# Scores of the early odd units written to the feed-forward banks, early maxima moved to one tile of their own

## The chip, the core and the metric

The kernel runs on one core of a Trainium2 chip. The core has a matmul engine (PE, with a separate weight-load track PEld), three engines for element-wise work (DVE, ACT, POOL), a queue engine (SP) that issues all transfers here, and DMA engines. The metric is the device time of one execution in microseconds, given as the median of several runs.

## What is computed

Pooled attention with 8 batches and 8 heads of 64 columns, followed by a feed-forward layer whose activation is `h * cos(h)`. Queries are averaged in pairs, so 576 pooled queries meet 1152 keys per head.

```python
def _attn_ref(q, k, v):
    B, H, S, D = q.shape                      # 8, 8, 1152, 64
    q_pool = q.reshape(B, H, S // 2, 2, D).mean(axis=3)
    scores = np.matmul(q_pool, k.transpose(0, 1, 3, 2)) / np.sqrt(D)
    scores = scores - np.max(scores, axis=-1, keepdims=True)
    attn = np.exp(scores)
    attn = attn / (np.sum(attn, axis=-1, keepdims=True) + 1e-09)
    return np.matmul(attn, v)
...
    x = attn_out.transpose(0, 2, 1, 3).reshape(B * S // 2, H * D)   # 4608 x 512
    h = x @ w_in                                                    # w_in 512 x 2048
    return (h * np.cos(h)) @ w_out                                  # w_out 2048 x 512
```

## The kernel before, in words

**Pairs and units.** Heads are taken two at a time: 32 pairs, `p` = 0 to 31. Each pair has ten units of attention work, so 320 units `u`, with `p, i = divmod(u, 10)`. Nine units of a pair are wide: four matmuls of 512 columns write the scores of two blocks of 128 keys into one PSUM tile `st` of two banks (`s_unit`, L1217). One unit of a pair is the remainder (64 queries per head, many matmuls of 64 columns, `s_rem`, L1240), the sixth of a pair in the first three pairs and the first of a pair after that. After the scores ACT takes the exponential of the whole tile out of PSUM (`soft`, L1267), and one unit later PE multiplies the result by the values (`av`, L1293 and L1342), accumulating in `ava` and `avb`.

**Maxima.** The exponent needs the row maximum of the scores, which enters as an additional row of the second query part `q2T`. So before a pair's scores PE computes a cheaper version of them from `q1T` alone, DVE reduces it to maxima, ACT writes them beside the second query part (L991 or L1063), and a transposing DMA makes `q2T` (L994 or L1067). In the first three pairs (`NHW` = 3) this goes head by head: four calls of `head_main` and one `head_rest` per head, then `mx_mixed` and `mx_mixed_rest`. The last of these also spreads the value maximum of the pair, from which ACT scales the pair's values (`prep_v`, L1106) before its first `av`.

**Banks.** The kernel lays out eight PSUM banks of 512 fp32 columns: `st` and `mx` are one tile of two banks each, `f` is two tiles of one bank each, `ava` and `avb` are one bank each. A tile is reused in the order in which the program takes tiles of that name, once the last reader of the one before has finished. `f` is the bank of the feed-forward tiles; before the feed-forward starts it holds the weight maxima (`wam`), the third part of the remainder scores in the first four pairs, and some of the early maxima: with `NMXF` = 2, of the calls of `head_main` for pair 1 every second one (`two`) takes two `f` tiles instead of `mx`.

**Order.** The body is written once in program order. `arrange` then takes the recorded instructions and sets each engine's order by a list schedule: it keeps a clock per engine, costs for each instruction, and always places the ready instruction with the lowest place in the program. A change between matmul tile shapes adds a fixed cost on PE. Each engine works through its own order strictly, waiting on semaphores.

**Feed-forward.** Weights are loaded and decoded early (DVE L518, L521, L524, ACT L531, L558, L559, POOL L562). When the four pairs of a batch are done, its rows go through `ffn1` (L1553, into `f`) and `ffn2` (L1613), interleaved with the units of later pairs. Thirty-two pairs' units and 18 chunks of feed-forward work share PE from then on.

Of the kernel before, what the change touches and what calls it, by code (L numbers as in the profile page):

```python
# [9 lines left out]
F32 = mybir.dt.float32  # L10
# [4 lines left out]
AF = mybir.ActivationFunctionType  # L15
# [5 lines left out]
P = 128  # L21
# [29 lines left out]
SRATE = (1.0, 0.6)  # L51
EWR = 2
NMIX = 5
NMXF = 2
NREM = 4
SIN2 = 1
VACT = 6
# [87 lines left out]
def n_out(wr):  # L145
    return wr[0][2] if wr else 1


def arrange(tc, nc, extra, fill):
# [3 lines left out]
    for i in rec:  # L153
        rd, wr = boxes(i)
        eng = str(i.engine).split(".")[-1]
        if eng == "PE":
# [15 lines left out]
            c = max(n_out(wr) * 0.0004167 + 0.0025, 0.0295)  # L172
            if rd[0][4] == 4:
                c = 2 * max(n_out(wr) * 0.00167 + 0.0025, 0.112)
# [21 lines left out]
    for k, nd in enumerate(nodes):  # L196
        deps = set()
        for w, lst in ((0, nd["rd"]), (1, nd["wr"])):
            for t, box, *_ in lst:
                name = t.name  # L200
                if name not in hist:
                    hist[name] = ([], [], set())
                    tag = getattr(t, "tag", None)
# [39 lines left out]
    for a, b, *kind in extra:  # L243
        a, b = node_of[a], node_of[b]
# [35 lines left out]
    while total:  # L280
        best = None
        for e in engines:
            while wait[e] and wait[e][0][0] <= now[e]:
                heapq.heappush(avail[e], heapq.heappop(wait[e])[1])
            if avail[e]:
                cand = (now[e], avail[e][0], e)
            elif wait[e]:
                cand = (wait[e][0][0], wait[e][0][1], e)
            else:
                continue  # L290
            if best is None or cand < best:
                best = cand
        t0, (_, k), e = best
        if avail[e]:
            heapq.heappop(avail[e])
        else:
            heapq.heappop(wait[e])
        nd = nodes[k]
        if nd["lock"]:
            t0 = max(t0, lock)  # L300
        c = nd["cost"]
        if e == "Activation":
            f = "sin" if "Sin" in nd["func"] else "exp" if "Exp" in nd["func"] else table
            if f != table:
                c += 1.28
                table = f
        if e == "PE" and nd["tile"] != mode:
            c += 0.15
            mode = nd["tile"]
        end = t0 + c  # L310
        if nd["lock"]:
            lock = end
        now[e] = end
        fin = end + HAND.get(e, 0.06)
        if e == "SP":
            if nd["cost"] > 1.0:
                end = now[e] = max(end, dma_free - 1.0)
            dma_free = max(dma_free, end) + nd["dma"]
            fin = dma_free + nd["lat"]
        done[k] = fin  # L320
        order[e].append(k)
        total -= 1
        for j in users[k]:
            r = done[k] if nodes[j]["eng"] != e or e == "SP" else end
            if (k, j) in issue:
                r = end
            if nodes[j]["eng"] == "SP" and e != "SP":
                r += SPM
            ready[j] = max(ready[j], r)
            left[j] -= 1  # L330
            if not left[j]:
                heapq.heappush(wait[nodes[j]["eng"]], (ready[j], nodes[j]["key"]))
# [18 lines left out]
def tile_attention_ffn(  # L351
# [10 lines left out]
    nc = tc.nc  # L362
# [18 lines left out]
    exp_scale = 0.5 / math.sqrt(D)  # L381
    l_add = math.log(PMAX)
# [10 lines left out]
    psum = ctx.enter_context(tc.tile_pool(name="psum", bufs=1, space=PSUM))  # L393
# [243 lines left out]
    def kcol(n, t, j, h):  # L637
        if n == 0:
            return t[:, (h * KT + j) * P : (h * KT + j + 1) * P]
        js = J0 if j < RB else J1  # L640
        return kpart(t, js)[:, h, j - js.start]
# [114 lines left out]
    def mx_main(n, t, c):  # L756
        if n not in mxs:
            mxs[n] = sb2.tile([P, NSL, 3], F32, tag="mxs", name="mxs")
        mx_n[0] += 1
        two = n < NMXF and mx_n[0] % 2  # L760
        banks, m = first_tile(2, None if two else "mx")
# [79 lines left out]
    def head_main(h, t):  # L841
        def fn(n):
# [4 lines left out]
            mx_n[0] += 1  # L847
            two = n < NMXF and mx_n[0] % 2
            banks, whole = first_tile(2, None if two else "mx")
# [61 lines left out]
    def first_tile(two, main):  # L911
        if main:
            m = psum.tile([P, 2, 512], F32, tag=main, name="m0")
            return [m[:, 0], m[:, 1]], m
        return [psum.tile([P, 512], F32, tag="f", bufs=2, name="m0") for _ in range(two)], None
# [273 lines left out]
    st = {}  # L1189

    def jof(p, i):
        nf = nf_of(p)
        if not 0 < nf < KT:
            return i - 1
        n = min(nf, KT - nf)
        seq = [x for a in range(n) for x in (a, nf + a)]
        return (seq + list(range(n, nf)) + list(range(nf + n, KT)))[i - 1]

    def banks_of(p, i):
        if p < NHW:  # L1200
            x = 2 * (i if i < FREM else i - 1)
            return [divmod(y, KT) for y in (x, x + 1)]
        return [(h, jof(p, i)) for h in range(2)]

    def is_rem(p, i):
        return i == (0 if p >= NHW else FREM)

    def s_unit(u):
        if u >= NP * NU:
            return  # L1210
        p, i = divmod(u, NU)
        ka, kb, qa, qb = k1[p % 3], k2[p % 2], q1T[p], q2T[p]
        if not is_rem(p, i):
            s = psum.tile([P, 2, 512], F32, tag="st", name="st")
            for y, (h, j) in enumerate(banks_of(p, i)):
                for w, x, part in ((ka, qa, 0), (kb, qb, 1)):
                    nc.tensor.matmul(  # L1217
                        s[:, y, :].rearrange("p (t c) -> p t c", c=P),
                        kcol(p, w, j, h),
                        x[:, h * QT : (h + 1) * QT, :],  # L1220
                        start=part == 0,
                        stop=part == 1,
                        skip_group_check=True,
                    )
            st[u] = [(s.rearrange("p a c -> p (a c)"), 2 * 512)]
            return
        st[u] = [s_rem(p, 0, JR, "st")]

    def s_rem(p, j0, j1, tag):
        ka, kb, qa, qb = k1[p % 3], k2[p % 2], q1T[p], q2T[p]  # L1230
        if tag == "f":
            s = psum.tile([P, 512], F32, tag=tag, bufs=2, name=tag).unsqueeze(1)
        else:
            s = psum.tile([P, 2, 512], F32, tag=tag, name=tag)
        for j in range(j0, j1):
            r = j - j0
            for h in range(2):
                for w, x, part in ((ka, qa, 0), (kb, qb, 1)):
                    o = (r % RB) * P + h * D
                    nc.tensor.matmul(  # L1240
                        s[:, r // RB, o : o + D],
                        kcol(p, w, j, h),
                        x[:, 2 * QT + (h if part == 0 else 0), HALF[h]],
                        start=r % RB == 0 and h == 0 and part == 0,
                        stop=False,
                        skip_group_check=True,
                    )
        n = (j1 - j0) * P
        return s.rearrange("p a c -> p (a c)")[:, 0:n], n

    def soft(u):
        p, i = divmod(u, NU)
        nf = nf_of(p)
        src = st.pop(u)
        rem = is_rem(p, i)
        if rem:
            src.append(s_rem(p, JR, KT, "f" if p < NREM else "mx"))
        parts = {}
        j0 = 0 if rem or p < NHW else jof(p, i)
        for s, n in src:  # L1260
            js = range(j0, j0 + n // P) if rem else [j0]
            f = sum(j < nf for j in js)
            full = n > P
            tag = ("pp" if full else "pps") if f else ("e" if full else "es")
            nb = (NPP if f else NE) if full else 1
            e = sb2.tile([P, n], F32, tag=tag, bufs=nb, name=tag)
            nc.scalar.activation(e, s, AF.Exp, scale=exp_scale, bias=l_add)  # L1267
            pp, c0 = None, 0
            if f < len(js):
                c0 = f * P  # L1270
                tag = "pp" if full else "pps"
                pp = sb2.tile([P, 2, n], F16, tag=tag, bufs=NPP if full else 1, name=tag)
                nc.scalar.copy(pp[:, 0, c0:n], e[:, c0:n])  # L1273
                if full and u % DSH == DSH - 1 and u >= DFIRST:
                    nc.vector.tensor_sub(pp[:, 1, c0:n], e[:, c0:n], pp[:, 0, c0:n])  # L1275
                else:
                    for o in range(c0, n, 512):
                        c = slice(o, min(o + 512, n))
                        nc.gpsimd.tensor_sub(pp[:, 1, c], e[:, c], pp[:, 0, c])  # L1279
            for a, j in enumerate(js):  # L1280
                w = slice(a * P, (a + 1) * P) if rem else slice(0, n)
                parts[j] = (e[:, w], None) if j < nf else (pp[:, 0, w], pp[:, 1, w])
            j0 += n // P
        return parts
# [518 lines left out]
    for u in range(NUNITS):  # L1803
        p, i = divmod(u, NU)
# [12 lines left out]
        while credit > 0.0:  # L1817
            c = next(ffn, None)
# [74 lines left out]
```

## Time and profile before

| | us |
|---|---|
| median of 3 runs | 1529.35 (1526.34 to 1531.48) |
| the profiled execution | 1525.26 |
| its span, first to last instruction | 1523.4 |
| PE busy | 1490.2 (98% of the span) |
| ACT busy | 1172.4 (77%) |
| DVE busy | 1124.1 (74%) |
| POOL busy | 929.6 (61%) |

The span is read first: 1.9 us of the execution lie outside it. Busy time of PE overstates its work a little, since the shown length of one matmul includes the time its result takes to drain while the next already runs. So a wait on PE shows as idle time only for the part that is longer than that overlap. What ended an idle stretch is named behind an arrow.

### The profile page before, as it was taken

The page shows a single profiled execution, that of the slowest core. Times are in us where ns is not written, and L with a number is a line of the kernel's source. Part 1 is how long each engine was busy: PE and PEld are TensorE (multiplying, and loading weights), DVE is VectorE, ACT ScalarE, POOL GpSimd, SP SyncE. Part 2 cuts the span into 40 slices and gives each one's busy share as a digit, 9 for nine tenths or more (in the row PEclk, how much of TensorE's full clock was granted, in tenths as well). Part 3 has the DMA queues.
Part 4 walks back from the last instruction along what each step waited for, and adds up shares of the span by engine and source line. Part 5 has one row for each costly group of instructions (what it writes and reads, how often), then busy time and mean ns, then how long its engine had stood idle before and what let it go on. Part 6 is the DMA issues. An engine that isn't in the chain of part 4 may idle for free.

```text
span 1523.4 us, 39324 instructions
## 1 busy us (share of the span) xinstructions
PE 1490.2 (98%) x16774; PEld 1027.2 (67%) x16774; DVE 1124.1 (74%) x1556; ACT 1172.4 (77%) x1475; POOL 929.6 (61%) x806
## 2 busy tenths in 40 slices
PE   5999999999999999999999999999999999999998
PEld 3777787657666676666666657667666667666665
DVE  7898987777888788887867887878787875343332
ACT  4877689888988788887968887988888787864442
POOL 4644757886665858686555586676767665521222
PEclk9999999999999999999999999999999999999999
DMA  9978742635354433535333334454453321001000
GB/s 264 273 219 181 177 93 48 125 78 116 70 102 102 108 89 76 128 79 123 73 75 79 73 83 107 86 104 103 80 120 83 80 56 32 17 19 32 20 16 22
DMA packets 226111, 145.15 MB, mean 95 GB/s; under 512 B 202448, under 2 KB 204752, under 8 KB 223888
## 3 DMA queue, kind: packets, MB, share of 16 engines
q1 hardware_dynamic: 225936, 142.65, 40.5%
q8 instruction: 131, 2.15, 0.6%
q14 instruction: 44, 0.36, 0.1%
HBM read 74.45 MB, written 10.49 MB: 56 GB/s over the span
## 4 chain that ended last, share of the span: by engine, by line
PE 88%; DVE 5%; ACT 3%; issue 1%; DMA 1%; POOL 1%; SPq 0%; ACTq 0%; DVEq 0%; POOLq 0%
PE f L1553 20%; PE f L1613 19%; PE st L1217 15%; PE ava L1293 8%; PE avb L1293 6%; PE m L765 6%; PE st L1240 2%; PE mx L1613 1%; DVE mxs L779 1%; PE ava L1342 1%; PE st L1553 1%; PE mx L808 1%; PE mx L787 1%; PE avb L1553 1%; PE mx L1553 1%
## 5 line engine op out<-in xcount | busy, mean ns | idle before, releaser
L1279 POOL TENSOR_TENSOR pp<-e,pp 128x512 f16<-128x512 f32 x374 | 457.3, 1244 | 270.6 <-ACT pp L1273 141.9
L1553 PEld LDWEIGHTS <-w 128*128 128x128 f16 x3456 | 331.4, 98 | 61.7 <-issue 3.0
L1553 PE MATMUL f<-xT,w 128*128 128x256 f16 x3048 | 366.2, 273 | 0.3 <-DVE y L1581 0.2
L1267 ACT ACTIVATE e<-st 128x1024 f32<-128x1024 f32 x267 | 272.5, 1020 | 109.9 <-PE st L1217 84.1
L779 DVE TENSOR_REDUCE mxs<-m 128x2 f32<-128x1024 f32 x232 | 283.2, 1221 | 97.1 <-PE m L765 95.0
L1613 PE MATMUL f<-w,g 128*128 128x512 f16 x1440 | 333.2, 380 | 0.7 <-DVE y L1581 0.7
L1503 POOL TENSOR_TENSOR g<-hsc,g 128x512 f16<-128x512 f32 x144 | 192.0, 1355 | 162.1 <-ACT g L1502 160.4
L1273 ACT CAST pp<-e 128x1024 f16<-128x1024 f32 x267 | 278.9, 1045 | 9.8 <-PE ava L1293 2.1
L1293 PEld LDWEIGHTS <-pp 128*128 128x128 f16 (+1 forms) x7062 | 238.8, 100 | 64.2 <-issue 12.5
L1613 PEld LDWEIGHTS <-g 128*128 128x128 f16 x1680 | 158.5, 98 | 177.3 <-DVE y L1581 0.9
L1217 PE MATMUL st<-q1T,k 128*128 128x512 f16 x576 | 218.8, 380 | 4.4 <-ACT pp L1267 4.1
L1293 PE MATMUL ava<-vc,pp 128*128 128x65 f16 (+5 forms) x4502 | 218.9, 198 | 1.3 <-DVE lx L1407 1.2
L1217 PE MATMUL st<-q2T,k 128*128 128x512 f16 x576 | 218.5, 379 | 0.0
L1293 PE MATMUL avb<-vc,pp 128*128 128x65 f16 (+1 forms) x3052 | 179.3, 197 | 0.0
L1217 PEld LDWEIGHTS <-k 128*128 128x128 f16 x1152 | 104.8, 98 | 100.9 <-issue 11.2
L1491 DVE TENSOR_TENSOR hsc<-hsc,y 128x512 f32<-128x512 f32 x144 | 134.8, 976 | 25.3 <-ACT y L1485 25.1
L1577 ACT ACTIVATE hsc<-f,small 128x512 f32<-128x512 f32 x127 | 86.7, 683 | 83.6 <-PE f L1553 83.2
L1581 DVE SCALAR_TENSOR_TENSOR y<-f,r1a,y 128x512 f32<-128x512 f32 x127 | 94.6, 745 | 66.1 <-ACT y L1580 61.3
L765 PE MATMUL m<-k,q1T 128*128 128x512 f16 x464 | 138.1, 379 | 2.5 <-DVE mxs L779 2.0
L1275 DVE TENSOR_TENSOR pp<-e,pp 128x1024 f16<-128x1024 f32 x80 | 127.5, 1593 | 16.7 <-ACT pp L1273 16.2
L1502 ACT CAST g<-hsc 128x512 f16<-128x512 f32 x144 | 83.0, 613 | 11.6 <-PE f L1613 11.6
L696 POOL TENSOR_TENSOR kst<-kld,kst 128x1152 f16<-128x1152 f32 x30 | 75.5, 2516 | 20.9 <-ACT kst L695 20.9
(189 smaller groups left out, 1853.6 us busy)
## 6 DMA issues: line engine op xcount, KB each, us to landing
vld<-in_v_dram SPq DMA_DIRECT2D x32, 576.0 KB, 3.8
kld<-in_k_dram SPq DMA_DIRECT2D x30, 576.0 KB, 4.5
qld<-in_q_dram SPq DMA_DIRECT2D x30, 576.0 KB, 4.6
k<-k SPq DMA_DIRECT2D x31, 288.0 KB, 3.5
wraw<-in_moe_w_in_dram SPq DMA_DIRECT2D x8, 1024.0 KB, 8.0
wraw<-in_moe_w_out_dram SPq DMA_DIRECT2D x8, 1024.0 KB, 6.1
out_dram<-ob SPq DMA_DIRECT2D x32, 256.0 KB, 2.4
left<-lx SPq DMA_DIRECT2D x64, 16.0 KB, 2.0
```

The lines of the kernel that those rows point to most:

```text
L765: nc.tensor.matmul(banks[h], q1T[n][:, h * QT + t, :], kmain(n, k1[n % 3], c, h), start=True, stop=True, skip_group_check=True,),
L779: nc.vector.reduce_max(mxs[n][:, t : t + QT + 1 : QT, c], m, axis=AX.X)
L1217: nc.tensor.matmul(s[:, y, :].rearrange("p (t c) -> p t c", c=P), kcol(p, w, j, h), x[:, h * QT : (h + 1) * QT, :], start=part == 0, stop= ...
L1267: nc.scalar.activation(e, s, AF.Exp, scale=exp_scale, bias=l_add)
L1273: nc.scalar.copy(pp[:, 0, c0:n], e[:, c0:n])
L1275: nc.vector.tensor_sub(pp[:, 1, c0:n], e[:, c0:n], pp[:, 0, c0:n])
L1279: nc.gpsimd.tensor_sub(pp[:, 1, c], e[:, c], pp[:, 0, c])
L1293: mm = nc.tensor.matmul(out, w, x, start=start, stop=False, skip_group_check=True)
L1491: nc.vector.tensor_mul(hj, hj, y[:, j : j + 2])
L1503: nc.gpsimd.tensor_sub(gt[:, 1], hj, gt[:, 0])
L1553: mm = nc.tensor.matmul(ps[:, fi, :], w1[wt][:, hp, fs], ck.xT[hp][:, xi, cs], start=n == 0, stop=n == 3 * HP - 1, skip_group_check=True,)
L1613: nc.tensor.matmul(po, gt[:, gi, f % 2, ts_], w2[wt][:, f, :], start=f == 0 and (gi, wt) == (0, 0), stop=f == NF - 1 and (gi, wt) == (1, 0),)
```

## The change

Three things change in the source.

- Units 1, 3, 5 and so on to 49 (`LENT`) take two `f` tiles of one bank for their scores instead of one `st` tile of two banks. The remainder units among them (5, 15 and 25) are not touched, which leaves 22 units. Since the two banks are now separate tiles, their exponential is two ACT instructions of 512 columns instead of one of 1024.
- `NMXF` goes from 2 to 0: all maxima of pair 1 go through the one `mx` tile.
- In `arrange` a change of matmul tile shape costs 0.1 instead of 0.15.

```diff
-NMXF = 2
+NMXF = 0
+LENT = range(1, 50, 2)
...
         if e == "PE" and nd["tile"] != mode:
-            c += 0.15
+            c += 0.1
...
         if not is_rem(p, i):
-            s = psum.tile([P, 2, 512], F32, tag="st", name="st")
+            if u in LENT:
+                s = [psum.tile([P, 512], F32, tag="f", bufs=2, name="sf") for _ in range(2)]
+            else:
+                t = psum.tile([P, 2, 512], F32, tag="st", name="st")
+                s = [t[:, 0], t[:, 1]]
...
-                        s[:, y, :].rearrange("p (t c) -> p t c", c=P),
+                        s[y].rearrange("p (t c) -> p t c", c=P),
...
-            st[u] = [(s.rearrange("p a c -> p (a c)"), 2 * 512)]
+            st[u] = [(s if u in LENT else [t.rearrange("p a c -> p (a c)")], 2 * 512)]
...
-            nc.scalar.activation(e, s, AF.Exp, scale=exp_scale, bias=l_add)
+            w = n // len(s)
+            for a, b in enumerate(s):
+                nc.scalar.activation(
+                    e[:, a * w : (a + 1) * w], b, AF.Exp, scale=exp_scale, bias=l_add
+                )
```

All numbers of matmuls stay the same; what moves is their order. In the rows below a tile's number is its place in the program; lines of the changed kernel are one higher up to L1211 and up to nine higher behind it.

PE before, at the first two units (`warm` are filler matmuls that wait for nothing, `st_338` and `st_345` the scores of units 0 and 1, `ava_385` the values of unit 0, `m0_231` the first maxima of pair 1):

```order
L1217 MATMUL st_338<-q2T_161,k2_0_69 128x512
...
L974 MATMUL m0_210<-k1_0_92,q1T_109 128x128
...
L613 MATMUL warm_277<-ident_85 128x128
...
L1217 MATMUL st_345<-q2T_161,k2_0_69 128x512
L1342 MATMUL ava_385<-vc_0_75,pp_343 128x65 x8
...
L852 MATMUL m0_231<-k1_1_93,q1T_227 128x512
```

PE after, at the same place (`sf_342` and `sf_343` are the two halves of unit 1, `st_366` is unit 2):

```order
L1222 MATMUL st_335<-q2T_161,k2_0_69 128x512
...
L1222 MATMUL sf_342<-q2T_161,k2_0_69 128x512
...
L1222 MATMUL sf_343<-q2T_161,k2_0_69 128x512
...
L1222 MATMUL st_366<-q2T_161,k2_0_69 128x512
...
L1351 MATMUL ava_383<-vc_0_75,pp_340 128x65 x8
...
L853 MATMUL m0_231<-k1_1_93,q1T_227 128x512
```

The scores of unit 2 have moved ahead of the values of unit 0.

DVE before, at the last maxima of pair 1 (`mx_413` is the rest of its second head, `mx_419` the mixed part, `mx_441` the last part with the value maximum, `w2_1` the weight being decoded, `sv` the value scale):

```order
L889 TENSOR_REDUCE mxs_230<-mx_413 128x4
L524 SCALAR_TENSOR_TENSOR w2_1_84<-wraw_398,w2_1_84 128x1024
L817 TENSOR_REDUCE mxs_230<-mx_419 128x2
L518 TENSOR_SCALAR w2_1_84<-wraw_466 128x1024
L835 TENSOR_REDUCE mxs_230<-mx_441 128x1
L837 TENSOR_REDUCE amx_446<-mx_441 128x1
L433 TENSOR_SCALAR amx_446<-amx_446 128x1
L441 TENSOR_SCALAR small_77<-amx_446 128x1
L990 TENSOR_REDUCE m_450<-mxs_230 128x5
L1098 RECIPROCAL sv_580<-small_77 128x1
L1099 TENSOR_SCALAR sv_580<-sv_580 128x1
```

DVE after, at the same place:

```order
L890 TENSOR_REDUCE mxs_230<-mx_412 128x4
L1403 TENSOR_TENSOR xp_729<-avb_555,rs_739 128x4x64
L522 SCALAR_TENSOR_TENSOR w2_1_84<-wraw_635,w2_1_84 128x1024
L818 TENSOR_REDUCE mxs_230<-mx_418 128x2
L525 SCALAR_TENSOR_TENSOR w2_1_84<-wraw_635,w2_1_84 128x1024
L836 TENSOR_REDUCE mxs_230<-mx_441 128x1
L838 TENSOR_REDUCE amx_446<-mx_441 128x1
L434 TENSOR_SCALAR amx_446<-amx_446 128x1
L442 TENSOR_SCALAR small_77<-amx_446 128x1
L991 TENSOR_REDUCE m_450<-mxs_230 128x5
L1099 RECIPROCAL sv_581<-small_77 128x1
L1100 TENSOR_SCALAR sv_581<-sv_581 128x1
```

The reductions of pair 1's last maxima now stand behind the closing of pair 0's values (`xp_729`) and behind the third weight's decoding; before they stood ahead of both.

PE after, between the rest of pair 1's second head and the first values of pair 1 (`sf_704` is half of unit 11, `sf_786` and `sf_787` are unit 13, `m0_504` belongs to pair 2):

```order
L880 MATMUL mx_412<-k1_1_93,q1T_227 128x128
...
L1222 MATMUL sf_704<-q2T_353,k2_1_70 128x512
...
L1222 MATMUL sf_786<-q2T_353,k2_1_70 128x512
...
L809 MATMUL mx_418<-k1_1_93,q1T_227 64x512
...
L1222 MATMUL sf_787<-q2T_353,k2_1_70 128x512
...
L825 MATMUL mx_441<-k1_1_93,q1T_227 128x128
...
L853 MATMUL m0_504<-k1_2_94,q1T_409 128x512
L1351 MATMUL ava_769<-vc_1_76,pp_701 128x65 x8
```

Before, `mx_441` stood in the values of unit 5 and the first values of pair 1 followed five units later; now one pair of matmuls lies between the two.

PE before, from pair 3's last maxima to its first scores (`mx_1201` the last maxima, `f_1468` the first scores that read its `q2T_1264`; the `avb_1309` rows are the values of three units):

```order
L824 MATMUL mx_1201<-k1_0_92,q1T_788 128x128
...
L1217 MATMUL st_1366<-q2T_709,k2_0_69 128x512
...
L1342 MATMUL avb_1309<-vc_0_75,pp_1364 128x65 x8
...
L1217 MATMUL st_1389<-q2T_709,k2_0_69 128x512
...
L1342 MATMUL avb_1309<-vc_0_75,pp_1387 128x65 x8
...
L1240 MATMUL f_1468<-q2T_1264,k2_1_70 128x64
```

PE after, at the same place:

```order
L1351 MATMUL avb_1325<-vc_0_75,pp_1432 128x65 x8
...
L825 MATMUL mx_1217<-k1_0_92,q1T_795 128x128
...
L766 MATMUL m0_1276<-k1_1_93,q1T_1169 128x512
...
L766 MATMUL m0_1317<-k1_1_93,q1T_1169 128x512
...
L766 MATMUL m0_1342<-k1_1_93,q1T_1169 128x512
...
L1245 MATMUL st_1435<-q2T_1280,k2_1_70 128x64
```

The scores and values that lay between have moved ahead of `mx_1217`; three maxima of pair 4 remain, each in the one `mx` tile.

## Rows read from the trace of the kernel before

**Rows 1.** The page's chain that ended last, shares by engine.

```profile
PE 88%; DVE 5%; ACT 3%; issue 1%; DMA 1%; POOL 1%; SPq 0%; ACTq 0%; DVEq 0%; POOLq 0%
```

**Rows 2.** Windows: length, busy PE PEld DVE ACT POOL (count), clock, DMA share, GB/s.

```profile
32.00:182.00 150.00, 142.88 (x1372) 110.83 (x1371) 137.10 (x218) 109.64 (x145) 84.12 (x82) 1.00 0.83 220
182.00:600.00 418.00, 415.89 (x5069) 288.17 (x5066) 339.23 (x459) 357.46 (x440) 298.76 (x258) 1.00 0.43 92
```

**Rows 3.** Waits of PE, 25 to 182 us: in total, times, longest.

```profile
PE st L1217 <- ACT pp L1267: 4.1, 8, 1.1
PE m L852 <- DMA q1T<-q1s: 1.5, 1, 1.5
PE mx L879 <- DVE mxs L863: 0.9, 1, 0.9
PE st L1240 <- ACT pp L1267: 0.8, 1, 0.8
PE m L765 <- DVE mxs L779: 0.6, 1, 0.6
PE mx L787 <- DVE mxs L779: 0.6, 1, 0.6
```

**Rows 4.** Timeline of PE, 25 to 32 us: start, length, what, idle before.

```profile
25.39 0.38 PE L1217 MATMUL st<-q1T,k 128*128 128x512 f16 x1
...
28.39 1.90 PE L1342 MATMUL ava<-vc,pp 128*128 128x65 f32 x16
31.79 1.04 PE L852 MATMUL m<-k,q1T 128*128 128x512 f16 x4 [1.50 <-DMA q1T<-q1s]
```

**Rows 5.** Groups by line up to 182 us: busy, mean ns of one, idle before.

```profile
L863 DVE TENSOR_REDUCE mxs<-m 128x1 f32<-128x1024 f32 x12 | 14.6, 1217 | 1.9 <-PE m L852 1.9
L889 DVE TENSOR_REDUCE mxs<-mx 128x4 f32<-128x512 f32 x4 | 2.7, 684 | 0.8 <-PE mx L879 0.8
L521 DVE SCALAR_TENSOR_TENSOR w<-wraw,w 128x1024 uint32<-128x1024 uint32 x8 | 10.3, 1288 | 0.1
L1267 ACT ACTIVATE pp<-st 128x1024 f32<-128x1024 f32 x44 | 44.9, 1021 | 28.3 <-PE st L1217 24.9 <-PE st L1240 3.1
L558 ACT ACTIVATE w<-w,wsc 128x1024 f32<-128x1024 f32 x8 | 9.2, 1144 | 1.0 <-DVE wsc L550 1.0
L559 ACT CAST w<-w 128x1024 f16<-128x1024 f32 x8 | 8.3, 1043 | 0.2
L1267 ACT ACTIVATE pps<-f 128x128 f32<-128x128 f32 x4 | 1.1, 273 | 1.4 <-PE f L1240 1.4
```

**Rows 6.** Timelines of DVE, ACT and PE, 51 to 64 us, pair 1.

```profile
51.38 0.28 DVE L835 TENSOR_REDUCE mxs<-mx 128x1 f32<-128x128 f32 x1
...
52.47 0.15 DVE L1099 TENSOR_SCALAR sv<-sv 128x1 f32<-128x1 f32 x1
...
53.63 1.24 ACT L1106 ACTIVATE vc<-vld,sv 128x1152 f32<-128x1152 f32 x1
...
63.56 0.63 PE L1342 MATMUL ava<-vc,pp 128*128 128x65 f32 x4
```

**Rows 7.** Timelines of PE and SP at pair 3, 118 to 125 us.

```profile
118.27 0.28 PE L824 MATMUL mx<-k,q1T 128*128 128x128 f16 x2
...
120.74 1.30 SPq L1067 DMA_TRANSPOSE q2T<-qs  x1
...
124.92 0.19 PE L1240 MATMUL f<-q1T,k 128*128 128x64 f16 x1
```

**Rows 8.** Transfers issued, 100 to 200 us: count, median us to landing.

```profile
q2T<-qs SPq DMA_TRANSPOSE x3, 3.8
```

**Rows 9.** Line L1553, the first feed-forward product: min/median/max ns, first and last start.

```profile
L1553 PE MATMUL f<-xT,w x3048: 269/273/284, 182.4 to 1485.3; 128*128 128x256 f16 x191
```

**Rows 10.** The start of PE (timeline) and the end of the span (window, columns of Rows 2).

```profile
12.04 1.89 PE L923 MATMUL m<-k,q1T 128*128 128x512 f16 x4 [12.04 <-DMA q1T<-q1s]
...
1500.00:1523.40 23.40, 19.43 (x138) 13.23 (x136) 1.54 (x3) 0.00 (x0) 3.29 (x3) 0.98 0.12 34
```

More of the change, by code (lines that the diff above doesn't have):

```diff
@@ L1248, in s_rem @@
         n = (j1 - j0) * P
-        return s.rearrange("p a c -> p (a c)")[:, 0:n], n
+        return [s.rearrange("p a c -> p (a c)")[:, 0:n]], n
     def soft(u):
```

## The prediction

> **What bounds the kernel now.** I read the chain of waits first: 88% of the span is PE [rows 1]. Then the windows: from 182 us, where the first feed-forward product runs [rows 9], to 600 us PE is busy for 415.9 of 418 us, while from 32 to 182 us it is busy for 142.9 of 150 us [rows 2]. The number of matmuls does not change, so the end moves by what PE loses or stops losing in waits, and nearly all that the change can touch lies ahead of 182 us: the last lent unit is 49, and the feed-forward, which needs the four pairs of units 0 to 39 and a few steps behind them, starts about there. The other engines there are not idle either: DVE 137.1 and ACT 109.6 of 150 us [rows 2]. DVE, at 91%, is nearly as full as PE.
>
> Third, PE's own waits in that stretch [rows 3]: nine for an exponential (`st` tile still being read), 4.1 + 0.8 = 4.9 us; three for a reduction of maxima, 0.9 + 0.6 + 0.6 = 2.1 us; one of 1.5 us for the transposed queries of pair 1. The shown idle time is too small for each wait: a matmul of 512 columns lasts 0.38 us in the trace, yet four of them end within 1.04 us, so they follow each other (1.04 - 0.38) / 3 = 0.22 us apart [rows 4], and the first 0.16 us of a wait hides under the drain of the matmul before it.
>
> **What the change takes away.** With alternate units in other banks, the next writer of a score tile stands two units behind, so the nine waits for the exponential can go: 4.9 + 9 x 0.16 = 6.3 us. One of them, at unit 1, lies ahead of the wait for pair 1's queries and so was worth nothing by itself: PE would have reached that 1.5 us wait earlier [rows 4]. There the gain is instead that unit 2's scores, 4 x 0.22 = 0.9 us, are pulled into the waiting time. The two about balance, so 6.3 stands. Of the reduction waits (2.1 + 3 x 0.16 = 2.6 us) I let 1.2 us go, since the order around them changes but the single `mx` tile stays. Together 7.5 us taken away; between 4 (half of the exponential waits come back as others) and 8.9 us.
>
> **What it adds on ACT.** Twenty-two units pay two half-wide exponentials. No such row exists; between 128 columns at 0.273 us and 1024 at 1.021 us [rows 5] a straight line gives 0.273 + 384/896 x 0.748 = 0.594 us (estimate), so 2 x 0.594 - 1.021 = 0.17 us for each, 3.7 us in all. ACT idles 28.3 us ahead of just these exponentials, waiting for PE [rows 5], and that covers it; uncovered it would cost at most its 3.7 us. I take nothing.
>
> **What it adds at pair 1.** All twelve maxima steps of pair 1 now go one after the other through the one `mx` tile, each waiting for its reduction on a DVE that is also decoding weights. Before, the value scale of pair 1 was ready at 53.63 + 1.24 = 54.87 us and its first use came at 63.56 us, 8.7 us to spare [rows 6]. In the new order that slack is gone: behind `mx_412` PE has only `sf_704`, `sf_786`, `mx_418`, `sf_787`, `mx_441` and `m0_504` ahead of the first values of pair 1, that is five tiles of two full matmuls' time, 5 x 0.43, and three matmuls of 128 columns, at a quarter of 0.22 each 0.17: 2.3 us of work. The chain that must run meanwhile, in DVE's order: reduce `mx_412` 0.68, one decoding step 1.29, reduce `mx_418` 1.22, another decoding step 1.29 [rows 5], then from the reduction of `mx_441` to the scale 52.62 - 51.38 = 1.24, then ACT 1.24 [rows 6]. Sum 7.0 us, so PE idles 7.0 - 2.3 = 4.7 us. Less if one decoding step finishes early (3.5); more if `sf_787` also waits for the exponential of `sf_704`, which stands behind two weight steps of ACT, 1.14 + 1.04 [rows 5] (6).
>
> **At pair 2** the same pattern, shorter: behind the mixed maxima `mx_804` there are sf, st and maxima matmuls of 7 x 0.43 + 0.17 = 3.2 us ahead of pair 2's first values; the chain is 1.22 + 1.24 + 1.24 = 3.7 us, and on ACT two weight steps of 1.14 + 1.04 stand ahead of the scaling [rows 5, 6]. So 0.5 us if ACT runs them early, 2.7 us if not. I take 2.0, since in ACT's new order they stand directly ahead of it.
>
> **At pair 3** the queries are late. Before, 118.27 us (last maxima) to 120.74 us (transpose issued) is 2.5 us, the landing takes 3.8 us more [rows 7, 8], together 6.3 us, and PE had 124.92 - 118.27 = 6.65 us of scores and values in between, so nothing was lost. Now PE has `mx_1217` and three maxima, 0.17 + 3 x 0.43 = 1.5 us, and those each wait for the `mx` tile. Idle: 4.8 us by these rows; 3.5 if the ACT step is prompter than it was there. I take 4.2.
>
> **The sum.** Added 4.7 + 2.0 + 4.2 = 10.9 us (7.5 to 13.5), taken away 7.5 us (4 to 8.9). Net +3.4 us. Behind 182 us the order is reshuffled too, but PE waits there for only 2 us in 418 [rows 2]; I put 0 with 2 us either way. Span 1523.4 + 3.4 = 1526.8 us; the execution lies 1.9 us above its span, 1528.7 us against 1525.26. That execution was 4.1 us under the median of the runs shown, 1529.35, so on the median the forecast is 1532.8, rounded to 1533 us. The bounds give 7.5 - 8.9 - 2 = -3.4 and 13.5 - 4 + 2 = +11.5 us, so 1526 to 1541.
>
> **The rivals.** About 0.3% (4.6 us) is what a measurement of this kernel can tell from no change.
>
> *Slower: the lent banks wait too.* The two `f` banks are not free for the asking: weight maxima and the third part of the remainder sit in the same ring, and their reader is DVE, or ACT behind weight steps. If a lent half waits for such a reader as often as `st` waited for an exponential, less than 6.3 us of gain remains and the gaps at the three pairs stand nearly alone: 10.9 - 3 = +7.9 us, about 1537. It decides from the point where the exponential and `f` waits together still come to more than 5 us. For it: DVE is 91% busy in the stretch [rows 2]. Against it: sixteen weights taken two at a time make eight weight maxima, against 22 lent units. Chance 0.30.
>
> *Slower: the clock falls in a gap.* From 32 to 600 us the granted clock is 1.00 [rows 2]; in the last stretch, where PE runs out of work, it is 0.98 [rows 10], and at the start, after 12 us without work, four matmuls of 512 columns took 1.89 us, against 1.04 us for the same four later [rows 10, 4]. The gaps at pairs 1 and 3 would be the longest since the start; the longest wait so far, 1.5 us, cost no clock that these rows show [rows 3, 2]. One fall priced like the start, where the slow stretch ended by 25.4 us at the latest [rows 4], is at most half of 13.4 us, +6.7 us on top of the sum: up to 1540. Chance 0.06. The Trainium skill, TensorE: Matmul & The Clock Gate, Part 1, states that half rate is the engine's default and that idleness brings it back; this trace shows it at both ends and nowhere between, so by that page the gaps could cost more than their length.
>
> *Faster: the gaps fill.* PE reaches the boundaries of pairs 1 to 3 later than the maxima need, because it has taken more scores first, and DVE, which then waits for PE less, runs its decoding steps ahead. If the three gaps shrink to 3 us in all, 3 - 8.9 = -5.9 us, 1523.5. It decides when the first values of pair 1 wait less than 1.5 us. For it: DVE does wait for maxima now and then (1.9 us at L863 [rows 5]). Against it: in DVE's fixed order the decoding steps stand between pair 1's last reductions, so they cannot run ahead of them. Chance 0.20.
>
> **How the numbers follow.** Forecast, within 0.3% and on its slow side: 0.44; slower by either mechanism 0.36; faster 0.20. So faster by over 0.3% 0.20, within 0.3% 0.44, slower by over 0.3% 0.36. The range reaches into the faster case, to 1523, and to the upper bound, 1541; outside it I leave about 0.1 at either end.
>
> **What would show it.** PE's waits for L1267 up to the feed-forward fall from 4.9 us to under 1.5. A wait of PE ahead of the first values of pair 1, released by ACT's scaling of `vc`, 2 us or longer, with more idle just ahead of it at the `mx` matmuls; a wait of PE at the first remainder scores of pair 3 released by the `q2T` transpose or by DVE. The first feed-forward product starts later than 182.4 us plus the work it now has ahead of it. If the waits at pairs 1 and 3 are under 1 us each, the prediction is wrong towards faster; if new waits of `sf` for DVE add up to over 3 us, towards slower.

## The result, and the profile after

The changed kernel takes 1541.68 us (median, 1540.59 to 1543.27) against 1529.68 us for the kernel before beside it: ratio 1.0091, 95% interval 1.0067 to 1.0116. It is 12.0 us slower. The forecast was 1533 us with a range of 1526 to 1541, so the time lies just outside it. The profiled execution took 1540.81 us, with a span of 1538.6 us, 15.2 us more than the span before.

The waits of PE ahead of the feed-forward, the view of [rows 3], now read:

```profile
PE m L766 <- DVE mxs L780: 2.7, 2, 1.4
PE sf L1222 <- ACT pp L1274: 1.8, 1, 1.8
PE m L766 <- DVE amx L838: 1.4, 2, 0.8
PE m L766 <- DVE sv L1100: 1.4, 1, 1.4
PE ava L1351 <- ACT vc L1107: 1.2, 1, 1.2
PE m L853 <- DVE amx L838: 1.0, 1, 1.0
PE m L853 <- DMA q1T<-q1s: 0.4, 1, 0.4
```

They sum to 9.9 us in nine waits. Before it was 9.0 us in fourteen: the 8.5 us of [rows 3] and one more of 0.5 us for an exponential. The waits have changed places and hardly their sum, so the loss is not in them. It is in a column beside them. Windows of the changed kernel (columns of [rows 2]):

```profile
32.00:182.00 150.00, 140.38 (x1165) 108.55 (x1164) 121.19 (x189) 97.62 (x144) 70.20 (x72) 0.89 0.75 202
63.60:80.60 17.00, 15.66 (x64) 12.91 (x64) 11.98 (x15) 9.41 (x16) 8.31 (x8) 0.50 0.84 285
107.98:118.10 10.12, 10.12 (x45) 8.63 (x43) 6.02 (x6) 4.64 (x7) 7.47 (x10) 0.50 0.66 228
142.10:148.80 6.70, 5.38 (x44) 3.00 (x44) 5.34 (x9) 3.08 (x5) 1.96 (x5) 0.50 1.00 300
```

From 32 to 182 us PE is busy nearly as much as before (140.4 against 142.9 us), yet it gets through 1165 matmuls instead of 1372, at a granted clock of 0.89 instead of 1.00. (The count is a hint only: matmuls differ in size, and the order has moved some of them across 182 us.) Three stretches hold all of the fall of the clock: each was granted 0.50, the level of 1.2 GHz instead of 2.4. PE is busy in them for 15.66 + 10.12 + 5.38 = 31.2 us, and half of it, 15.6 us, is work that full clock would have saved. Behind 182 us little changed. The windows from there to the end are, before and after:

```profile
182.00:1523.40 1341.40, 1331.06 (x15294) 905.84 (x15290) 965.11 (x1308) 1047.20 (x1307) 829.58 (x685) 1.00 0.35 78
```

```profile
182.00:1538.60 1356.60, 1345.65 (x15487) 918.06 (x15485) 980.90 (x1333) 1060.95 (x1327) 838.23 (x695) 1.00 0.35 79
```

PE is not busy for 10.3 us there before and for 10.9 us after. So about nothing from the waits (0.9 us as shown, 0.1 us once the 0.16 us that each hides is counted), 15.6 us of slow clock and 0.6 us behind make up the 15.2 us of the span to within about 1 us.

The clock falls where PE keeps running out of work. PE's timeline at the boundary of pair 1 (start, length, what, idle before):

```profile
59.62 0.62 PE L809 MATMUL mx<-k,q1T 128*64 128x512 f16 x4
62.04 0.38 PE L1222 MATMUL sf<-q1T,k 128*128 128x512 f16 x1 [1.80 <-ACT pp L1274]
62.26 0.38 PE L1222 MATMUL sf<-q2T,k 128*128 128x512 f16 x1
...
63.77 1.01 PE L853 MATMUL m<-k,q1T 128*128 128x512 f16 x2 [0.97 <-DVE amx L838]
65.95 3.65 PE L1351 MATMUL ava<-vc,pp 128*128 128x65 f32 x16 [1.17 <-ACT vc L1107]
...
77.83 0.63 PE L1222 MATMUL st<-q1T,k 128*128 128x512 f16 x1
78.25 0.63 PE L1222 MATMUL st<-q2T,k 128*128 128x512 f16 x1
```

Two scores of 512 columns start 0.22 us apart at 62.04 us, and 0.42 us apart at 77.83 us, where nothing waits: the second pair runs at half clock. At pairs 2 and 3 the same view shows:

```profile
105.00 0.59 PE L766 MATMUL m<-k,q1T 128*128 128x512 f16 x2 [0.81 <-DVE amx L838]
106.96 0.59 PE L766 MATMUL m<-k,q1T 128*128 128x512 f16 x2 [1.37 <-DVE mxs L780]
...
140.13 0.59 PE L766 MATMUL m<-k,q1T 128*128 128x512 f16 x2 [0.58 <-DVE amx L838]
142.08 1.01 PE L766 MATMUL m<-k,q1T 128*128 128x512 f16 x2 [1.35 <-DVE sv L1100]
144.41 1.01 PE L766 MATMUL m<-k,q1T 128*128 128x512 f16 x2 [1.32 <-DVE mxs L780]
145.22 0.26 PE L1245 MATMUL st<-q1T,k 128*128 128x64 f16 x1
```

Each of these maxima waits for the reduction of the one ahead of it in the single `mx` tile; the row that names `sv` does too, since on DVE that small step ends at 142.08 us, right behind a reduction that ran from 140.82 us for 1.21 us. Read in finer windows, the clock falls at 63.6 us, inside the second wait of pair 1; at 108.0 us, half a microsecond into the values behind the second wait of pair 2; and at 142.1 us, as the second wait of pair 3 ends. The last waits shown at pairs 1 and 3 (1.17 and 1.32 us) already lie in the slow stretch.

### The profile page after: what moved, and what is told of

Same layout as the page of the kernel before. It is cut to its first block, busy times and chain, and to the rows that moved or that the text cites. A ratio compares the mean times of both kernels' runs of the same rounds, so it can differ in the third digit from the quotient of the medians.

```text
span 1538.6 us, 39341 instructions
## 1 busy us (share of the span) xinstructions
PE 1503.6 (98%) x16774; PEld 1037.8 (67%) x16774; DVE 1124.8 (73%) x1552; ACT 1175.2 (76%) x1497; POOL 925.0 (60%) x810
## 5 line engine op out<-in xcount | busy, mean ns | idle before, releaser
L1222 PE MATMUL st<-q1T,k 128*128 128x512 f16 x532 | 202.7, 381 | 1.3 <-ACT e L1274 1.2
L1222 PE MATMUL st<-q2T,k 128*128 128x512 f16 x532 | 202.6, 381 | 0.0
L1511 ACT CAST g<-hsc 128x512 f16<-128x512 f32 x144 | 83.3, 613 | 10.6 <-PE f L1622 10.6
```

The source lines that it names most:

```text
L1222: nc.tensor.matmul(s[y].rearrange("p (t c) -> p t c", c=P), kcol(p, w, j, h), x[:, h * QT : (h + 1) * QT, :], start=part == 0, stop=part == 1,
```

## The experiments

Two theories stood against each other. A: the single `mx` tile bunches the maxima at the pair boundaries, PE idles there, and the clock halves behind each bunch. B: the lent banks and the new order cost the time, or DVE and ACT set the pace there, so that the slow clock only fills time that PE would have waited anyway.

### Matmuls put into the gaps

If the clock is the cost, work that nobody needs should make the kernel faster, as long as it lies in the gaps. It is the most direct test, and it was made twice: in the gaps of pairs 1 and 2, and in those of all three pairs. `GAPS` gives, for a pair, places counted from its last maxima (-1 is one step ahead of them) and how many matmuls go there; they multiply the identity into columns that are overwritten or never read.

```diff
+GAPS = {1: ((-1, 30), (1, 16), (2, 18)), 2: ((1, 13), (2, 22)), 3: ((1, 10), (2, 22), (3, 22))}
...
+                    mm = nc.tensor.matmul(
+                        ta[:, 0:P], ident, ident, start=True, stop=True, skip_group_check=True
+                    )
```

Pairs 1 and 2:

> The changed kernel with matmuls of 128 columns that wait for nothing new, put into the gaps on PE: 64 ahead of the first values of pair 1 (30, 16 and 18 in its three waits), 35 at the boundary of pair 2 (13 and 22 in its two waits); their results are written to unused columns and never read. Nothing is put in at pair 3. Theory A (the cost is the clock): the stretches at 0.5 behind the boundaries of pairs 1 and 2 go, the one behind pair 3 stays; 8.2 + 5.3 = 13.5 us of work at half rate come back, less up to 5 us where PE then waits for DVE, 1528 to 1534 us. Theory B (DVE and ACT set the pace there, and the slow clock only fills what would have been waiting): PE waits longer instead, 1538 to 1543 us, clock or no clock.

Measured: 1532.17 us, ratio to before 1.0033 (1.0021 to 1.0046), inside theory A's range and 6 us under theory B's. The stretches behind pairs 1 and 2 are gone. The one behind pair 3, where nothing was put in, remains and is shorter:

```profile
136.00:139.30 3.30, 2.81 (x39) 2.26 (x39) 2.75 (x8) 0.12 (x2) 1.84 (x4) 0.50 0.85 292
```

All three pairs, with the changed kernel beside it on the same chip:

> The changed kernel as it is, beside the next three on the same chip. By its earlier ratio of 1.009 it should come to 1539 to 1544 us, with stretches at 0.5 behind the boundaries of pairs 1, 2 and 3. Were the slow clock an accident of one execution, some executions would be near 1530 with a mean clock of 0.998 or more.

> The kernel with matmuls in the gaps of pairs 1 and 2, and now also at pair 3: 10, 22 and 22 ahead of the three maxima there that wait, written to columns that the next scores overwrite. Theory A (what the change costs beyond its idle time is the clock): the stretch at 0.5 behind pair 3 goes too, 1528 to 1533 us, that is 0 to 3 us under the kernel with two pairs filled and 2 to 5 us over before, which would be the idle time and the extra matmuls alone. Theory B (DVE and ACT set the pace): no faster than with two pairs filled, 1532 us or more.

Measured: the changed kernel 1541.91 us (1.0097, interval 1.0081 to 1.0112), with the same three stretches; with the gaps of three pairs filled 1531.09 us (1.0030, interval 1.0019 to 1.0041). 153 matmuls whose results nobody reads make the kernel 10.8 us faster. The window of the filled kernel, and its timeline at pair 1 (its lines stand 12 or more further down: L821 is the mixed maxima, L1337 the added matmuls, L1378 the first values):

```profile
32.00:182.00 150.00, 144.62 (x1436) 112.70 (x1435) 128.88 (x201) 105.69 (x155) 79.86 (x78) 1.00 0.80 217
```

```profile
60.32 0.62 PE L821 MATMUL mx<-k,q1T 128*64 128x512 f16 x4
60.88 1.85 PE L1337 MATMUL ava<-ident 128*128 128x128 bf16 x30
62.74 0.38 PE L1235 MATMUL sf<-q1T,k 128*128 128x512 f16 x1
...
64.90 1.17 PE L1337 MATMUL ava<-ident 128*128 128x128 bf16 x18
66.65 1.97 PE L1378 MATMUL ava<-vc,pp 128*128 128x65 f32 x16 [0.58 <-ACT vc L1120]
```

The clock is 1.00. From the mixed maxima to the first values of pair 1 it takes 66.65 - 60.32 = 6.33 us, and without the added matmuls 65.95 - 59.62 = 6.33 us: here they ran entirely inside the gap and changed only the clock. Theory B falls in its second form: when the clock is held, the time comes back. It was the filling of two pairs that decided this; the third pair, whose stretch held only 2.81 busy us by then, made no clear difference (1.0030 against 1.0033, on two chips). What remains over before is 4.1 us by the medians (2.9 to 6.3 by the interval). The waits account for it: the filled kernel shows 5.4 us of waits of PE from 25 to 182 us, in nine, with 9 x 0.16 = 1.4 us hidden, and 153 added matmuls about 0.056 us apart are 8.6 us; together 15.4 us, against 9.0 + 14 x 0.16 = 11.2 us before.

### The parts one by one

`NMXF = 0` alone:

```diff
-NMXF = 2
+NMXF = 0
```

> The kernel before with NMXF = 0 alone: all maxima of pair 1 through the one mx tile, no lent banks, shape changes still priced 0.15. Theory A (the single mx tile makes PE idle at the boundaries of pairs 1 to 3, and the granted clock then halves behind each gap): in the planned order the last maxima stand as close together at pairs 1 and 3 as in the changed kernel, so gaps of 8 to 12 us and two or three stretches at 0.5, 1545 to 1558 us. Rival B (the lent banks and the order around them cost the time, the slow clock comes with them): no stretch at 0.5, within 3 us of before, 1527 to 1533 us.

Measured: 1538.67 us, 1.0076 (1.0064 to 1.0089). That is between the two: the gaps and the slow clock are there without any lent bank, but smaller than A expected. Windows and the longest wait up to 182 us:

```profile
67.10:73.80 6.70, 6.70 (x28) 5.21 (x27) 4.72 (x5) 2.38 (x4) 4.69 (x6) 0.50 1.06 367
135.30:145.50 10.20, 7.49 (x50) 3.59 (x49) 8.10 (x20) 3.24 (x5) 2.21 (x5) 0.50 1.08 286
```

```profile
PE ava L1342 <- ACT vc L1106: 2.0, 1, 2.0
```

The first stretch begins where the first values of pair 1 have waited 2.0 us for their scale. Half of 6.70 + 7.49 is 7.1 us. The rest is waiting: PE's waits from 25 to 182 us sum to 15.4 us here, against 9.0 us before. 7.1 + 6.4 = 13.5 us, of the 15.0 us by which the span of this execution (1538.4 us) is longer than before's; by the medians the loss is 11.5 us. So by itself the one `mx` tile costs about as much in idle time as in clock.

Lent banks and the price, with `NMXF` back at 2:

```diff
-NMXF = 0
+NMXF = 2
```

> The changed kernel with NMXF = 2 again: lent banks and the shape price 0.1 stay, every second early maximum of pair 1 takes two f tiles as before. Theory A: the gaps at the pair boundaries and all three stretches at 0.5 go, what the lent banks remove stays, 1519 to 1527 us, granted clock 1.00 throughout. Rival B: still 1538 us or more, with stretches at 0.5. The lent halves and the early maxima share the two f tiles in units 1 to 9; waits of PE for f or sf there over 5 us would bring it to 1530 or more without any fall of the clock.

Measured: 1533.61 us, 1.0037 (1.0025 to 1.0050). Theory A expected a gain and a clock of 1.00 throughout, and missed both. The windows of the slow clock, and the waits at the second and third of them:

```profile
35.10:41.80 6.70, 5.77 (x17) 2.10 (x16) 5.43 (x8) 4.16 (x8) 4.54 (x3) 0.50 1.02 268
59.00:62.30 3.30, 3.30 (x22) 2.26 (x19) 2.60 (x3) 1.52 (x3) 3.30 (x3) 0.50 0.91 306
99.90:103.20 3.30, 3.23 (x10) 1.74 (x10) 2.86 (x5) 1.65 (x5) 2.13 (x3) 0.50 1.14 253
```

```profile
58.26 0.59 PE L853 MATMUL m<-k,q1T 128*128 128x512 f16 x2 [1.92 <-DVE mxs L864]
99.97 1.01 PE L766 MATMUL m<-k,q1T 128*128 128x512 f16 x2 [1.32 <-DVE mxs L780]
```

The falls have moved: the first lies in units 1 to 9, where lent scores and pair 1's maxima share the two `f` tiles and PE waits for DVE again and again (0.2 to 0.8 us each from 32 to 36 us). The other two stand at one wait each, of 1.92 and 1.32 us, with no other wait in the 3 us ahead of it. Half of 5.77 + 3.30 + 3.23 is 6.2 us, about the whole loss of 6.5 us. So the lent banks are no gain there, and what they cost is again the clock.

The price alone (0.15 to 0.1), and both other parts without it:

> The kernel before with the price of a shape change at 0.1 instead of 0.15 and nothing else. Both theories: the planned order at the pair boundaries is as before, no stretch at 0.5, within 3 us of before, 1527 to 1533 us.

Measured: 1529.06 us, 1.0014 (1.0003 to 1.0024): in time as expected, nearly nothing. In the trace not: one stretch stands at 0.50 behind a wait of 1.39 us, which neither theory had expected.

```profile
172.12 0.61 PE L787 MATMUL mx<-k,q1T 128*128 128x128 f16 x8 [1.39 <-DVE mxs L779]
```

```profile
172.80:176.00 3.20, 3.20 (x15) 2.08 (x15) 3.10 (x6) 0.00 (x0) 0.26 (x1) 0.50 0.81 256
```

> Lent banks and NMXF = 0 with the price of a shape change left at 0.15. In the planned order the maxima at pairs 1 to 3 stand as close together as in the changed kernel or closer. Theory A: the gaps and the stretches at 0.5 stay, 1539 to 1550 us. Rival (the price of 0.1 moved the steps that matter): 1533 us or less.

Measured: 1548.65 us, 1.0145 (1.0127 to 1.0163), with three stretches at 0.50 at the same boundaries. The price of 0.1 is no part of the loss; with the other two it saves some 7 us. The lent banks are part of it: beside `NMXF = 0` alone they raise the ratio from 1.0076 to 1.0145, at the same price. Most of that is again the clock: PE is busy for 26.7 us at 0.50 in this trace, against 14.2 us with `NMXF = 0` alone, while its waits sum to about the same (14.5 and 15.4 us).

### Where the lent banks pay

`LENT` begins later, at unit 11 (shown), 21 or 31; `NMXF` is 2, the price 0.1:

```diff
-LENT = range(1, 50, 2)
+LENT = range(11, 50, 2)
```

> The changed kernel with NMXF = 2 and the lent banks only from unit 11 on, so that lent scores and pair 1's early maxima hardly meet in the two f tiles. In the planned order the last maxima of pair 2 stand close together, those of pairs 1 and 3 don't. Theory A (the time follows the gaps at boundaries with bunched maxima, and the clock behind them): one gap of 2 to 4 us with one stretch at 0.5 about pair 2, against about 3 us of waits for exponentials that go: 2 us faster to 5 us slower than before. Rival B (lent banks cost by themselves): 5 us slower or more, with waits of PE for sf spread over all units from 11 to 49.

> The same with the lent banks from unit 21 on. In the planned order no last maxima of pairs 1 to 3 are bunched. Theory A: no stretch at 0.5, the waits for exponentials from unit 21 to 49 go (about 3 us before): 1 to 5 us faster than before. Rival B: 3 us slower or more.

> The same with the lent banks from unit 31 on. Theory A: no stretch at 0.5, some of the waits for exponentials go (about 2 us before): 0 to 4 us faster than before. Rival B: 2 us slower or more.

Measured: 1530.52 us (1.0017, 1.0007 to 1.0028), 1531.87 us (1.0028, 1.0017 to 1.0039) and 1521.72 us (0.9960, 0.9946 to 0.9975). The time of the first is as A expected, but its trace holds two stretches at 0.50 instead of one: 3.07 busy us from 101.7 to 105.0 us and 2.82 from 170.0 to 173.2 us, the second behind a wait of 2.38 us for a reduction. The second version is not as A expected: it is 3.8 us slower, the time that rival B named, and a stretch at 0.50 stands at 100.3 us, behind waits that A had not seen in the order. PE's timeline there, in the kernel lent from unit 21 on:

```profile
99.84 0.23 PE L466 MATMUL wam<-ident,wmx 128*128 128x128 bf16 x1 [1.49 <-ACT w L532]
100.88 0.29 PE L466 MATMUL wam<-ident,wmx 128*128 128x128 bf16 x1 [0.81 <-ACT w L532]
```

PE stands at the weight maxima until ACT has a weight ready. That the lent scores shifted these steps against each other is argued, not shown. Of B's mechanism little shows: PE waits for `sf` tiles for 0.5 us in all. The third version beats both kernels, and before by 6.4 us, more than the 0 to 4 us expected. It too has a stretch at 0.50 that A had ruled out, behind 182 us and behind one wait of 1.06 us:

```profile
185.40 0.59 PE L766 MATMUL m<-k,q1T 128*128 128x512 f16 x2 [1.06 <-DVE mxs L780]
```

```profile
187.00:190.20 3.20, 3.20 (x17) 2.28 (x16) 2.40 (x3) 1.87 (x2) 2.09 (x2) 0.50 1.00 242
```

The lent banks of this version by themselves:

> Lent banks from unit 31 on with NMXF = 2, and the price of a shape change at 0.15 as before: the lent banks alone. If the gain of the kernel lent from unit 31 on comes from the banks, 1519 to 1525 us; if it came from the price of 0.1, 1526 to 1531 us, no different from before.

Measured: 1524.45 us, 0.9980 (0.9969 to 0.9990). So the banks gain without the price too; the price may add to it. Part of the gain is in the waits ahead of 182 us: those for an exponential on `st` wide tiles fell from the 4.1 us of [rows 3] to 2.4 us in the kernel with the price of 0.1:

```profile
PE st L1222 <- ACT pp L1274: 2.4, 6, 0.8
```

All waits of PE there fell from 9.0 to 7.8 us. The profiled executions lie only 1.3 us apart (1523.99 and 1525.26 us), so where the rest of the 6.4 us between the medians comes from stays open.

### One long gap by itself

In the kernel before, three stalls were put where PE is otherwise full:

```diff
+STALL = {113: 1, 173: 2, 233: 4}
...
+                for r in range(STALL[u]):
+                    d = nc.vector.reduce_max(
+                        x[:, r * 16 : r * 16 + 1], s.rearrange("p a c -> p (a c)"), axis=AX.X
+                    )
```

> The kernel before with three stalls of PE put into the stretch that is otherwise full, ahead of the scores of units 114, 174 and 234: there PE runs nothing until a chain on DVE (1, 2 and 4 reductions of 1024 columns and one copy, all extra work) has read the scores just written. Nothing is computed differently. From the rows of the reductions (1.22 us each) the stalls should last about 2, 3 and 5.5 us, 10.5 us in all. Theory A1 (one gap is enough if it is long): the clock halves behind the stall of 5.5 us and that of 3 us, not or only sometimes behind that of 2 us, and each fall costs 2 to 8 us more than the stall: 1542 to 1552 us. Theory A2 (a fall needs several waits close together, as at the pair boundaries): no stretch at 0.5, the stalls cost their length, 1536 to 1539 us.

Measured: 1547.98 us, 1.0135 (1.0116 to 1.0155). The waits at the three places (3.34, 3.82 and 6.01 us, here in one row), and the windows of the slow clock, which begin inside them:

```profile
PE st L1245 <- ACT e L1313: 13.2, 3, 6.0
```

```profile
461.80:468.50 6.70, 5.69 (x42) 3.55 (x43) 3.62 (x5) 3.43 (x4) 0.00 (x0) 0.50 0.39 116
714.40:721.10 6.70, 4.98 (x45) 2.98 (x46) 4.53 (x8) 2.39 (x3) 0.00 (x0) 0.50 0.64 176
1004.50:1011.20 6.70, 3.61 (x37) 2.87 (x38) 6.67 (x6) 2.36 (x3) 6.68 (x5) 0.50 0.16 31
```

Even the shortest came to 3.3 us, since the next scores also wait for the exponential, which ACT starts only when the added reductions are done; of the planned stalls none was as short as 2 us. All three halved the clock, so a lone long gap suffices. A fourth stretch was not planned. It lies at the wait for pair 1's queries, which took 1.50 us before [rows 4] and 1.85 us here; the four maxima behind it take 1.89 us instead of 1.04 us.

```profile
31.85 1.89 PE L879 MATMUL m<-k,q1T 128*128 128x512 f16 x4 [1.85 <-DMA q1T<-q1s]
```

```profile
31.70:35.10 3.40, 3.25 (x8) 1.20 (x9) 2.50 (x3) 0.03 (x1) 0.00 (x0) 0.50 0.99 306
```

So, as far as these traces tell, a fall needs no bunch of waits and no long one. Waits of 1.06, 1.32, 1.39, 1.85 and 1.92 us, each with no other within the 2.7 us ahead of it, stand at falls or just ahead of them in the traces shown here, while the wait of 1.50 us in the profiled execution of before stands at none. What decides between them was not found.

The three waits at the stalls, 13.2 us, half of the 14.28 us busy at 0.50 behind them, 7.1 us, and half of the fourth stretch, 1.6 us, make 21.9 us. The span of this execution is 1544.6 - 1523.4 = 21.2 us longer than before's; by the medians it is 19.9 us. This is how a gap that brings the clock down is to be priced: its length, and half of what PE runs before the clock is back.

## Why the prediction was wrong

**What failed** is the step that left the clock out of the sum. "The clock falls in a gap" stood beside the sum as a rival, with a chance of 0.06 and a price of one fall of at most 6.7 us. It came three times, at just the three boundaries where the sum had put gaps. Its 31.2 busy us at 0.50 are 15.6 us of work, of which 10.8 us came back when the gaps were filled. Of the other 4.8 us about 4 show as waits of PE and added matmuls, which came to 15.4 us with the clock held against 9.9 + 9 x 0.16 = 11.3 us in the changed kernel; how much of it is DVE catching up while PE is slow and how much is added matmuls that overshoot was not measured. The reason for 0.06 was that the longest wait of before, 1.5 us, had cost no clock. It was one wait, and the experiments have single waits from 1.06 to 1.92 us at which, or just behind which, the clock did fall. In the changed kernel it fell at pairs of waits of 0.58 to 1.80 us, with less than a microsecond of matmuls between them; that waits so close together bring it down more surely than single ones is argued, not shown. And it was one execution: of 23 executions of the kernel before beside the last experiments, four had a mean clock of 0.997 and took 1529.6 to 1532.3 us, fourteen one of 1.000 and took 1523.3 to 1527.5 us; the other five, at 0.999, took 1525.6 to 1529.2 us. So the clock seems to fall in some executions of the kernel before too, though no trace of one was kept, and the profiled execution did not show it.

**The rule that was weighed.** The Trainium skill, TensorE: Matmul & The Clock Gate, Part 1, has half rate as the engine's default, to which idleness returns it; the section "A second HAM failure mode: psum-queue depth-cycling" of the same page adds, from another kernel, that frequent short idle times between groups of matmuls also make the clock go back and forth. The traces agree with both: 0.50 at a lone wait of 3.3 us, and at pairs of waits of 0.6 to 1.8 us. The prediction cited the first and took the 0.06 from the trace of before; the second can be read as a warning against a change that collects small waits in one place.

**The gap at pair 1**, 4.7 us by the prediction: the shown waits 1.80 + 0.97 + 1.17 and three times 0.16 us are 4.4 us. The chain was the one worked out, with decoding steps between the reductions; it left out the closing of pair 0's values, which DVE runs there in about 0.3 us. The 1.80 us is the wait of the unit's second half for the exponential of the one ahead. It had been named as the upper case, 6 us, and added nothing: it ran beside DVE's chain, whose last decoding step ended only at 63.32 us. The wait for `vc` itself was 1.17 us, not the 2 us or more that was to show it.

**Pair 2**, 2.0 us: 0.81 + 1.37 + 0.32 = 2.5 us. The size was right, and the waits stand elsewhere: the maxima wait for reductions on DVE, not the values for ACT's weight steps. The predicted path was about as long, though. ACT ran both weight steps ahead of the scaling, as expected, and `vc` was ready at 106.14 + 1.24 = 107.38 us, 0.06 us before the first values.

**Pair 3**, 4.2 us: 0.58 + 1.35 + 1.32 + 0.48 = 3.7 us. Again the maxima wait in the one `mx` tile, and the first scores, which were to wait for `q2T`, start at 145.22 us without a wait. Its transpose was issued at 140.85 us and landed 3.2 us later, at 144.05 us; without the waits of the maxima PE would have waited for it some 3.3 us (estimate: 144.05 - 139.22 us, less the 1.5 us of work). So that the size was met is in part luck. In all 10.6 us against 10.9 us.

**What was taken away.** PE's waits for an exponential fell from 4.9 us in nine [rows 3] to 1.8 us in one, and that one belongs to the gap at pair 1. In the changed kernel's own trace all waits of before went but the one for pair 1's queries, 11.2 - 0.6 = 10.6 us, more than the 7.5 us forecast and more than its upper bound, 8.9. So there the gaps cost nothing net, against the forecast of 3.4 us. With the clock held the change costs 4.1 us, with what the added matmuls overshoot in it. The sum of idle times is borne out to some 3 us and no better, which is small beside the clock.

**ACT's halves.** Estimated at 0.594 us; measured:

```profile
L1274 ACT ACTIVATE pp<-sf 128x512 f32<-128x512 f32 x44 | 24.5, 591 | 8.6 <-PE ava L1351 4.1 <-PE sf L1222 4.0
```

**Behind 182 us**, 0 with 2 us either way: 0.6 us. The first feed-forward product starts at 205.0 us instead of 182.4 us [rows 9], later as expected.

**"The lent banks wait too"**, 0.30: in the changed kernel no `sf` waits for DVE ahead of 182 us. With `NMXF` at 2 the early maxima and the lent halves do meet, and what it costs comes mostly through the clock. **"The gaps fill"**, 0.20: they did not.

## What to carry to other kernels

Price a gap on PE twice: its length, and, where the clock falls, half of the matmul time up to where it is back at 1.00. Don't take a wait of 1 to 2 us as safe because one execution shows it at full clock. When a change only moves waits about, look at where they collect, and read the granted clock by windows before the waits. Matmuls that nobody reads, put into a gap that cannot be closed, tell at once how much of a loss is the clock.

## What the hardware showed unexpectedly

- The slow stretches differ in length: about 17.0 us behind pair 1, 10.1 us behind pair 2, 6.7 us behind pair 3, and 3.3 us in some experiments. In the longest PE ran fp32 values, with two maxima matmuls among them, without a pause from 65.95 to 76.97 us and was still at 0.50; the next scores of 512 columns began at 77.83 us and the clock was back at 80.6 us. Whether the kind of matmul matters was not tried.
- A wait of about a microsecond may be enough to bring the clock down: in the kernel lent from unit 31 on the only wait shown in the 9 us ahead of a fall is one of 1.06 us.
- At the start the column of the granted clock and the length of the matmuls disagree: in the kernel before it reads 1.00 from 12 to 21 us, although four matmuls of 512 columns took 1.89 us there, and 1.04 us later [rows 10, 4].
- 64 extra matmuls ahead of the first values of pair 1 delayed them by nothing (6.33 us either way), and 153 in all gave back 10.8 us.
